# Attention and a gated MLP on one core: landing times in the plan, gated loads, second buffers, another order of block sums

## The chip, the cores and the metric

One Trainium2 chip, one core of it. The metric is the device time of the core in microseconds, from the first to the last instruction and what lies around it. Lower is better.

## The reference

Attention of 8 batches of 8 heads, 576 rows, head size 64, with keys and values averaged over groups of 8 rows (so 72 keys); its output, as 4608 rows of 512, goes through a gated MLP with 1536 hidden columns.

```python
k_p = k.reshape(B, H, Sp, pool, D).mean(axis=3)
v_p = v.reshape(B, H, Sp, pool, D).mean(axis=3)
scores = scale * np.matmul(q, k_p.transpose(0, 1, 3, 2))
attn = softmax(scores)                       # with 1e-9 added to the sum
x = np.matmul(attn, v_p)                     # (4608, 512) after a transpose
g = x @ w_gate
out = (g / (1 + np.exp(-g)) * (x @ w_val)) @ w_out
```

All arrays are float32. The kernel keeps that precision by splitting operands into a high and a low 16-bit part and adding three products.

## The kernel before

**Tiling.** The 4608 rows are nine tiles of 512 rows, the 1536 hidden columns twelve chunks of 128. A step is one chunk of one tile: gate and value products of x with that chunk's weights, tanh, and the product of both, `h`.

**Three stages.** In the first (to about 184 us) the weights are loaded and split, and tile 0 is computed whole, with an order of instructions written out by hand (`ORDER`). In the second (184 to 752 us) tiles 1 to 8 run twelve steps each, `h` is stored to DRAM (`hd`, L1138), and the attention of batches 2 to 7 runs beside the steps, in pieces of up to 128 rows. In the third, the out stage (from 752 us), the stored `h` of two tiles at a time (a pair, four pairs) is multiplied by `w_out`.

**Two ways to do a step.** A plain step (`plain_step`, lines 1026 to 1028) has 24 matmuls of 512 columns. A fast step (`fast_step`, `product`, L1116) is a seven-product scheme: seven products of six matmuls of 256 columns, 42 in all, with three ACT copies (L1172, L1174, L1181) and two DVE sums (L1177, L1182) of partial sums. It needs sums of the chunk's weights, which `fast_weights` makes once per chunk for the first `FAST` = 9 chunks (DVE L1043, POOL L1049 and L1062, ACT L1055), and sums of x, `xc`, which `fast_x` makes once per tile after x has landed (DVE L1083, L1087 on DVE or POOL, ACT L1088, L1091). A tile takes a fast step when a chunk is converted and `xc` is due soon, else a plain one. Chunks 9 to 11 are always plain.

**Attention.** `prep(b)` prepares a batch: eight loads of 0.5 MB into three `mid` buffers (`sums`, `batch_load`, L582), their sums over groups of 8 (POOL L391 to L393, DVE L386) and largest values (DVE L445) into `home["ks"]` and `home["vs"]`, a scale, and the splits of keys and values (`split_k` L457, L459, `split_v` L477 to L486) into one of two boxes, which are shared by batches b and b - 2. A piece is asked for (`ask`: queries, L600) and answered (`answer`: scores L650 and L651, softmax, a turning DMA L1290, values L776 and L777, a second turning DMA into x, L1424). The second stage has 30 such pieces, and one of batch 1.

**What sets the order.** The second and third stages are planned while the program is built: `Order` runs generators ("lines") that each yield an operation with an engine, a cost in ns and a time from which it can start; `Order.run` takes the operation that can start first, with a rank of kinds (`KINDS`) where several can, and writes it to its engine's queue. Every engine then works in that order. Buffers are pools (`get`, `put`), results are flags (`done`, `flag`). Landing times of DMAs are added by hand, for instance `t + 2500` after the store of `h`, `t + 5500` after a batch load.

**The out stage.** `sums_of_w_out` makes seven sums of w_out's blocks, each cut into a high part (ACT L1473) and a low one (POOL L1474). Per pair, `load_block` loads four blocks of h over the weights that are no longer needed, `operands` forms block differences (DVE L1569) and cuts seven operands into high (ACT L1555) and low parts (L1559: thirds 0 and 2 on DVE, 1 on POOL), two operand sets in turn, and `last_products` multiplies them (PE L1642, L1656, L1657) with PSUM copies (L1593, L1614) and adds (L1620, L1626) between.

## Time and profile before

| | |
|---|---|
| runs of the kernel, us | 983.07, 986.18, 988.71 (median 986.18) |
| the profiled execution, us | 989.56 |
| its span, first to last instruction, us | 987.7 |
| PE / DVE / ACT / POOL busy, us | 902.9 / 754.0 / 552.4 / 500.0 |
| mean granted TensorE clock | 0.973 of full |
| DMA | 159.84 MB, mean 162 GB/s |

One execution is profiled, and its times start at its first instruction. Busy time counts an instruction from its start to its end; a matmul's end is modelled, so neighbouring matmuls overlap. Idle time of an engine is put down to what released it, found from semaphores. PE is TensorE, DVE VectorE, POOL GpSimd, SP the queue that issues the DMAs.

### The profile page before, as it was taken

What the parts mean: (1) busy time and instruction counts of PE and PEld (TensorE: products, weight loads), DVE (VectorE), ACT (ScalarE), POOL (GpSimd) and SP (SyncE); (2) the same over time, 40 slices, a digit from 0 to 9 for tenths busy, and PEclk for the clock granted to TensorE, in tenths of its full rate; (3) what the DMA queues carried; (4) which work ended last, traced back from release to release, by engine and by line L of the source; (5) the groups of instructions that cost most, each with busy time, mean ns of one, the idle gap of its engine ahead of it and who ended that gap; (6) DMA issues with size and microseconds to landing.
All of it is one profiled execution on the core that took longest, in us unless ns stands there. A gap on an engine that the chain in (4) does not pass through costs nothing. (4 is left out here: it accounts for less than half of the span.)

```text
span 987.7 us, 17119 instructions
## 1 busy us (share of the span) xinstructions
PE 902.9 (91%) x6368; PEld 590.6 (60%) x6368; DVE 754.0 (76%) x1157; ACT 552.4 (56%) x1033; POOL 500.0 (51%) x519
## 2 busy tenths in 40 slices
PE   6779998598998898998798999999999999999998
PEld 5557554344446646767556768778686555555554
DVE  5789865778987997987877876755468977788684
ACT  3778873264645746674756667754456444444442
POOL 4546448067667568666586544644355322232220
PEclk9989999799999999999898999999999999999999
DMA  9865543479659439569568384451437260805401
GB/s 350 249 174 202 208 150 73 130 228 234 130 160 222 130 108 258 155 136 242 165 161 239 112 165 122 122 139 66 128 121 284 90 252 22 292 27 183 158 22 64
DMA packets 176660, 159.84 MB, mean 162 GB/s; under 512 B 115392, under 2 KB 147136, under 8 KB 172992
## 3 DMA queue, kind: packets, MB, share of 16 engines
q1 hardware_dynamic: 176576, 158.74, 54.8%
q8 instruction: 50, 0.82, 0.4%
q14 instruction: 34, 0.28, 0.1%
HBM read 95.94 MB, written 37.75 MB: 135 GB/s over the span
## 5 line engine op out<-in xcount | busy, mean ns | idle before, releaser
L1656 PE MATMUL ps<-low,wsh 128*128 128x512 bf16 x336 | 127.0, 378 | 0.0
L1026 PE MATMUL ps<-x,wgv_h 128*128 128x512 f16 x312 | 121.3, 389 | 1.9 <-DMA x<-box 1.4
L1027 PE MATMUL ps<-x,wgv_h 128*128 128x512 f16 x312 | 120.9, 387 | 0.2 <-DVE x L791 0.2
L1028 PE MATMUL ps<-x,wgv_l 128*128 128x512 f16 x312 | 120.7, 387 | 0.0
L834 ACT ACTIVATE hf<-ps,un 128x512 f32<-128x512 f32 x96 | 65.8, 685 | 84.7 <-PE ps L1028 42.1
L1116 PEld LDWEIGHTS <-mixed 128*128 128x128 f16 x1026 | 99.7, 99 | 19.4 <-issue 5.7
L1116 PEld LDWEIGHTS <-wgv_h 128*128 128x128 f16 x912 | 88.6, 99 | 29.1 <-issue 15.7
L633 POOL TENSOR_TENSOR box<-qt,box 64x512 f16<-64x512 f32 (+1 forms) x60 | 64.1, 1069 | 79.8 <-ACT box L631 62.0
L837 DVE SCALAR_TENSOR_TENSOR hf<-hf,ps 128x512 f32<-128x512 f32 x96 | 65.4, 682 | 42.3 <-ACT hf L834 42.0
L1116 PE MATMUL ps<-xc,mixed 128*128 128x256 f16 x684 | 91.4, 275 | 3.7 <-ACT ps L1174 3.6
L1116 PE MATMUL ps<-xc,wgv_h 128*128 128x256 f16 x456 | 81.3, 276 | 11.0 <-DVE ps L1182 9.9
L842 DVE SCALAR_TENSOR_TENSOR hf<-ps,un,hf 128x512 f32<-128x512 f32 x96 | 71.3, 743 | 23.8 <-PE ps L1116 15.7
L1116 PE MATMUL ps<-x,wgv_h 128*128 128x256 f16 x456 | 80.9, 275 | 1.8 <-ACT rs L1172 1.6
L1419 POOL TENSOR_TENSOR box<-sc,box 128x512 f16<-128x512 f32 (+1 forms) x30 | 37.3, 1243 | 56.9 <-ACT box L1418 48.2
L1116 PE MATMUL ps<-xc,wgv_l 128*128 128x256 f16 x228 | 63.0, 276 | 0.0
L1116 PE MATMUL ps<-x,wgv_l 128*128 128x256 f16 x228 | 62.7, 275 | 0.0
L1656 PEld LDWEIGHTS <-wsh 128*128 128x128 bf16 x336 | 32.5, 97 | 44.1 <-issue 7.4
L1559 POOL TENSOR_TENSOR low<-wgv_h,more 128x1024 bf16<-128x1024 f32 x10 | 25.8, 2579 | 63.6 <-ACT more L1555 63.6
L629 ACT ACTIVATE qt<-qt,inv 128x512 f32<-128x512 f32 (+1 forms) x60 | 40.7, 678 | 27.8 <-DMA qt<-q_twice 27.7
L1028 PEld LDWEIGHTS <-wgv_l 128*128 128x128 f16 x312 | 31.1, 100 | 39.2 <-issue 3.7
L1026 PEld LDWEIGHTS <-wgv_h 128*128 128x128 f16 x312 | 31.4, 101 | 33.0 <-issue 2.2
L1559 POOL TENSOR_TENSOR low<-wgv_h,hs 128x1024 bf16<-128x1024 f32 x10 | 24.7, 2468 | 52.1 <-ACT hs L1555 52.1
(211 smaller groups left out, 2492.2 us busy)
## 6 DMA issues: line engine op xcount, KB each, us to landing
hd<-hf SPq DMA_DIRECT2D x96, 256.0 KB, 2.5
ws<-w_all SPq DMA_DIRECT2D x12, 1536.0 KB, 7.5
qt<-q_twice SPq DMA_DIRECT2D x48, 256.0 KB, 3.5
wgv_h<-hd SPq DMA_DIRECT2D x8, 1536.0 KB, 8.7
wgv_l<-hd SPq DMA_DIRECT2D x8, 1536.0 KB, 7.9
out_t<-ob SPq DMA_DIRECT2D x36, 256.0 KB, 2.1
in<-k_rows SPq DMA_DIRECT2D x12, 576.0 KB, 5.3
in<-q_rows SPq DMA_DIRECT2D x12, 576.0 KB, 6.5
```

What stands on the lines that cost most here:

```text
L629: nc.scalar.activation(qt, qt, AF.Copy, scale=inv[:, b, 0:1])
L633: nc.gpsimd.tensor_sub(o[rows], qt[rows], o[rows])
L834: nc.scalar.activation(hf, gate, AF.Tanh, scale=un[:, c, 0:1])
L837: nc.vector.scalar_tensor_tensor(out=hf, in0=hf, scalar=1.0, in1=gate, op0=ALU.add, op1=ALU.mult)
L842: nc.vector.scalar_tensor_tensor(out=out, in0=val, scalar=un[:, c, 2:3], in1=hf, op0=ALU.mult, op1=ALU.mult)
L1026: nc.tensor.matmul(o, wh, x["h"][:, j], start=(j == 0), stop=False)
L1027: nc.tensor.matmul(o, wh, x["l"][:, j], start=False, stop=False)
L1028: nc.tensor.matmul(o, wl, x["h"][:, j], start=False, stop=(j == NJ - 1))
L1116: nc.tensor.matmul(o, a, b, start=begin and j + n == 0, stop=j == HJ - 1 and n == 2, skip_group_check=True,)
L1419: tp = yield op("POOL", 1205, lambda: nc.gpsimd.tensor_sub(xt[:, DM:], o, xt[:, :DM]), tp)
L1559: lambda: on.tensor_sub(low[:, 2 * n : 2 * n + 2], src[:, 2 * n : 2 * n + 2], rows[n].bitcast(F32)),
L1656: nc.tensor.matmul(o, top[:, c], where[1][:, c], start=False, stop=False, skip_group_check=True)
```

## The change

- **Landing times.** An operation may carry a second time: `dma` lets a load or store end for its queue after 400 ns and for who needs it after a landing time (batch loads 6500, queries 4200, blocks 9000, `h` 3000). `turn`, for turning DMAs, also lets SP be held until the last landing so far, less a margin.
- **Loads let go one by one.** A batch load takes a token (`"load": [0, 0, 0]`); each turning DMA gives one back when SP is through with it, and so does `idle` when nothing else can go on.
- **Second buffers.** `ks` and `vs` of odd batches get their own room (tag `wo2`), so `prep(b)` waits for the split of b - 2 instead of b - 1. `un`, `mt`, `r` and `ri` get more buffers. The two `rs2` sums of the out stage go to query buffers, the second buffer of `f` into the same room.
- **FAST 9 to 12.** The low parts of w_out are kept in two tiles, 9 and 3 chunks; the first is reused for the weight sums of chunks 9 to 11.
- **Sums of w_out.** The cuts are lines of their own, three of seven low parts go to DVE, the order of loads and sums changes.
- **Block sums of pairs.** The differences are formed in another order and other blocks, as a line of their own beside the cuts; low parts: thirds 0 and 1 on POOL, 2 on DVE. A new kind `seed` ranks the copies and adds that start a PSUM bank before `cut` and `out`.

```diff
-FAST = 9
+FAST = 12
-KINDS = "step", "xsum", "answer", "prep", "ask", "sums", "wsum", "load", "cut", "out"
+KINDS = "step", "xsum", "answer", "prep", "ask", "sums", "wsum", "load", "seed", "cut", "out"
...
+    def dma(self, land, f, *after, ns=400):
+        return *self.op("SP", ns, f, *after), lambda at, end: (end, at + land)
+
+    def turn(self, ns, early, land, f, *after):
+
+        def times(at, end):
+            end = max(end, self.landed - early)
+            return end, end + land
+
+        return *self.op("SP", ns, f, *after), times
...
+            if first is None and self.idle():
+                continue
...
-            self.free[engine] = at + ns
-            self.go(e, at + ns + self.LAG[engine])
+            end = done = at + ns
+            if times:
+                end, done = times[0](at, end)
+                self.landed = max(self.landed, done)
+            self.free[engine] = end
+            self.go(e, done + self.LAG[engine])
...
-            "sc": [0, 1], "pt": [0, 1], "set": [],
+            "sc": [0, 1], "pt": [0, 1], "set": [], "load": [0, 0, 0],
...
     def sums(b, i, split):
 
         n, t0 = yield get("mid")
-        t = yield op("SP", 450, lambda: batch_load(b, i, n), t0)
+        _, t1 = yield get("load")
+        t = yield dma(6500, lambda: batch_load(b, i, n), t0, t1)
         ns = {0: 2700, 1: 2386, 2: 1484}[max(0, i // 2 - 1)]
-        t = yield op("DVE" if i >= 4 else "POOL", ns, lambda: batch_sum(b, i), t + 5500, split)
+        t = yield op("DVE" if i >= 4 else "POOL", ns, lambda: batch_sum(b, i), t, split)
...
-            split = yield flag(("split", b - 1))
+            split = yield flag("room" if b == SPLIT + 1 else ("split", b - 2))
...
-        tp = 2500 + (
-            yield op("SP", 1650, lambda: turn(m, half, pt, OLD // P if old else 2 * H), tp, t0)
-        )
+        tp = yield turn_op(1450, 500, 2600, lambda: turn(m, half, pt, OLD // P if old else 2 * H), tp, t0)
+        put("load", 0, order.free["SP"])
...
+        def cut(k, g, o, t):
+            hi, lo = (a[g] for a in wpart[k])
+            t = yield op("ACT", 610, lambda: nc.scalar.copy(hi, o), t)
+            eng, ns, on = ("DVE", 800, nc.vector) if k in (1, 7, 3) else ("POOL", 1320, nc.gpsimd)
+            t = yield op(eng, ns, lambda: on.tensor_sub(lo, o, hi.bitcast(F32)), t)
+            order.done(("w cut", k, g), t)
...
-        t = yield op("SP", 450, lambda: nc.sync.dma_start(out=block[h, n], in_=src), t)
-        order.done(("block", p, h, n), t + 8000)
+        t = yield dma(9000, lambda: nc.sync.dma_start(out=block[h, n], in_=src), t)
+        order.done(("block", p, h, n), t)
...
-                eng, ns, on = (("DVE", 1230, nc.vector), ("POOL", 2550, nc.gpsimd))[n == 1]
+                eng, ns, on = (("POOL", 2500, nc.gpsimd), ("DVE", 2000, nc.vector))[n == 2]
...
+        def sums():
+            t = max((yield ready(0, 0)), (yield ready(0, 1)))
+            t = yield from less(b12, b12, b11, t)
+            order.done(("T", p, 1), t)
+            t = max(t, (yield ready(1, 1)), (yield flag(("cut", p, 5))))
+            t = yield from less(b12, b22, b12, t)
+            order.done(("T", p, 2), t)
+            t = yield from less(b11, b12, b11, t, (yield flag(("cut", p, 1))))
+            order.done(("T", p, 3), t)
+            t = yield from less(b21, b21, b12, t, (yield flag(("cut", p, 2))))
+            order.done(("T", p, 4), t)
+            t = max(t, (yield flag(("cut", p, 6))))
+            order.done(("free", p, 0, 1), t)
+
+        order.start(("cut", p), sums())
+        for k, src, when, free in (
+            (1, b11, ("block", p, 0, 0), None), (5, b12, ("T", p, 1), None), (2, b21, ("block", p, 1, 0), None),
+            (6, b12, ("T", p, 2), None), (3, b22, ("block", p, 1, 1), (1, 1)), (7, b11, ("T", p, 3), (0, 0)),
+            (4, b21, ("T", p, 4), (1, 0)),
+        ):
+            t = yield from cut(k, src, (yield flag(when)))
+            order.done(("cut", p, k), t)
+            if free:
+                order.done(("free", p, *free), t)
...
-                    order.start(prio, f)
+                    order.start(("seed", p), f)
```

## Rows read from the trace of the kernel before

**Rows 1.** The page, part 1 (busy time of each engine, share of the span, instructions) and, of part 2, the granted TensorE clock in 40 slices.
```profile
PE 902.9 (91%) x6368; PEld 590.6 (60%) x6368; DVE 754.0 (76%) x1157; ACT 552.4 (56%) x1033; POOL 500.0 (51%) x519
...
PEclk9989999799999999999898999999999999999999
```

**Rows 2.** Busy time by stretch (the windows view): stretch and its length, then busy us (instructions) of PE, PEld, DVE, ACT and POOL, granted clock, DMA share, GB/s. Five tiles of the second stage, then the last three together, then one pair of the out stage.
```profile
184.00:270.50 86.50, 81.83 (x500) 40.24 (x499) 70.53 (x127) 46.17 (x92) 53.40 (x63) 0.94 0.69 174
270.50:345.50 75.00, 66.03 (x519) 41.69 (x518) 63.39 (x114) 44.61 (x103) 48.52 (x58) 0.98 0.65 169
345.50:418.00 72.50, 68.04 (x563) 47.18 (x562) 64.47 (x105) 42.34 (x86) 51.91 (x58) 0.98 0.67 174
418.00:487.00 69.00, 61.44 (x577) 47.35 (x575) 56.32 (x105) 45.20 (x105) 42.41 (x53) 0.98 0.72 188
487.00:570.60 83.60, 74.03 (x628) 54.70 (x629) 65.31 (x129) 52.97 (x118) 56.35 (x66) 0.92 0.63 163
570.60:752.00 181.40, 177.29 (x1585) 137.72 (x1584) 116.95 (x217) 106.14 (x230) 84.85 (x92) 1.00 0.49 137
...
842.10:900.30 58.20, 56.89 (x252) 31.21 (x252) 45.37 (x34) 26.05 (x31) 16.91 (x7) 1.00 0.39 145
```

**Rows 3.** Groups of instructions by line: line, engine, operation, tiles, shapes, count | busy us, mean ns of one | idle us of the engine before them, and what ended it.
```profile
L1116 PE MATMUL ps<-xc,wgv_h 128*128 128x256 f16 x456 | 81.3, 276 | 11.0 <-DVE ps L1182 9.9 <-DVE hf L842 0.8
...
L650 PE MATMUL ps<-box 128*128 128x72 f16 (+1 forms) x240 | 25.1, 204 | 7.7 <-DVE sc L661 5.8 <-POOL box L633 1.2 <-DVE sc L781 0.4
...
L1177 DVE TENSOR_TENSOR ps<-ps,rs 128x256 f32<-128x256 f32 x57 | 24.3, 427 | 18.7 <-PE ps L1116 15.4 <-ACT qt L629 3.0 <-ACT box L1418 0.2
...
L776 PE MATMUL ps<-box,pt 128*128 128x64 f16 (+1 forms) x240 | 19.0, 197 | 11.7 <-DMA pt<-half 10.2 <-DMA qt<-q_twice 1.5
```

**Rows 4.** The chain of work that ended last, around the end of tile 7: start us, length us, what (merged where alike).
```profile
669.93 17.79 PE ps L1116 x162
...
690.33 0.22 PE ps L1026
...
690.98 0.22 PE ps L1026
```

**Rows 5.** Busy time by stretch of the fast products alone (L1116, PE): stretch and its length, busy us (matmuls), clock, DMA share, GB/s. Tiles 2 and 4.
```profile
270.50:345.50 75.00, 25.55 (x210) 0.98 0.65 169
...
418.00:487.00 69.00, 45.76 (x378) 0.98 0.72 188
```

**Rows 6.** Instructions of one line, L1062 (the last pieces of a conversion, on POOL): count: shortest/median/longest ns, start of the first and the last in us.
```profile
L1062 POOL TENSOR_TENSOR wgv_l<-fw,wgv_h x9: 662/672/1651, 215.6 to 466.2; 128x256 f16<-128x256 f32 x9
```

**Rows 7.** The same view of the two lines that issue turning DMAs, L1290 and L1424 (time that SP takes to issue one).
```profile
L1290 SPq DMA_TRANSPOSE pt<-half x31: 1240/1639/6030, 208.7 to 662.2; - x31
...
L1424 SPq DMA_TRANSPOSE x<-box x30: 1192/1233/2905, 235.6 to 670.9; - x30
```

**Rows 8.** The timeline of SP: start us, length us, queue, line, operation, what, count.
```profile
287.70 0.61 SPq L582 DMA_DIRECT2D in<-v_main  x1
...
509.93 0.49 SPq L582 DMA_DIRECT2D in<-v_main  x1
510.47 0.43 SPq L582 DMA_DIRECT2D in<-k_rows  x1
510.94 0.43 SPq L582 DMA_DIRECT2D in<-v_main  x1
511.51 2.41 SPq L1424 DMA_TRANSPOSE x<-box  x1
...
516.43 4.75 SPq L1290 DMA_TRANSPOSE pt<-half  x1
```

**Rows 9.** The timeline of DVE, PE and POOL: start us, length us, engine, line, operation, what, shapes, count, and in brackets the idle time before and what ended it.
```profile
286.04 0.99 DVE L486 SCALAR_TENSOR_TENSOR box<-box,inv 8x256 f16<-8x256 f32 x1
...
290.69 0.80 DVE L486 SCALAR_TENSOR_TENSOR box<-box,inv 8x256 f16<-8x256 f32 x1
...
517.72 2.29 DVE L386 TENSOR_REDUCE box<-in 128x72 f32<-128x576 f32 x2 [1.72 <-DMA in<-k_rows]
...
491.52 0.61 PE L1026 MATMUL ps<-x,wgv_h 128*128 128x512 f16 x1 [1.36 <-DMA x<-box]
...
508.00 2.38 POOL L1091 TENSOR_TENSOR xc<-fx,xc 128x512 f16<-128x512 f32 x2
...
784.15 2.38 POOL L1559 TENSOR_TENSOR low<-wgv_l,more 128x1024 bf16<-128x1024 f32 x1 [4.73 <-ACT more L1555]
...
785.03 3.72 DVE L1559 TENSOR_TENSOR low<-wgv_l,more 128x1024 bf16<-128x1024 f32 x2
```

**Rows 10.** Instructions of one line, L486 (the last part of a batch's split of v), columns as in rows 6.
```profile
L486 DVE SCALAR_TENSOR_TENSOR box<-box,inv x12: 483/895/1315, 205.5 to 599.0; 8x256 f16<-8x256 f32 x12
```

**Rows 11.** The same view of four kinds of instruction: the low parts of w_out's sums (L1474); who waited for the add of L1620, and how long (us in total, times); the low parts of operands (L1559) on DVE and on POOL.
```profile
L1474 POOL TENSOR_TENSOR half<-wf,wsh x6: 1262/1271/1272, 709.7 to 748.1; 128x512 bf16<-128x512 f32 x6
...
  PE ps L1642: 4.9, 4
...
L1559 DVE TENSOR_TENSOR low<-wgv_h,hs x20: 1212/1901/3395, 750.0 to 945.4; 128x1024 bf16<-128x1024 f32 x20
...
L1559 POOL TENSOR_TENSOR low<-wgv_h,hs x10: 2387/2439/2790, 751.0 to 944.5; 128x1024 bf16<-128x1024 f32 x10
```

**Rows 12.** The page, part 6: DMA issues of the first operand blocks, count, KB each, median us from issue to landing.
```profile
wgv_h<-hd SPq DMA_DIRECT2D x8, 1536.0 KB, 8.7
```

More of the change, by code (lines that the diff above doesn't have):

```diff
@@ L1030, in attention_then_swiglu, with idle @@
     x_home, xc_home = {1: (xp, "x0")}, {}
+    def idle():
+        waiting = any(e["need"] == ("get", "load") for e in order.lines)
+        if waiting:
+            put("load", 0, order.now)
+        return waiting
+    order.idle = idle
     converting, reserved = set(), {}
@@ L1487, in sums_of_w_out @@
-            t6 = yield less(a11, a22, a11, max(t3, t5c))
-            t6c = yield from cut(6, a11, t6)
-            t3 = yield less(a12, a12, a11, max(t6c, t2))
-            t = yield from cut(3, a12, t3)
+                land[m, k] = yield dma(3800, lambda: nc.sync.dma_start(out=o, in_=src), t)
+            for k, o, at_ in ((4, a22, (1, 1)), (1, a11, (0, 0)), (2, a12, (0, 1))):
+                order.start(("wsum", k), cut(k, g, o, land[at_]))
+            t = max(land[1, 0], (yield flag(("w cut", 4, g))))
@@ L1669, in last_products @@
             if k == 5:
-                where_f, trs = yield get("f")
-                rs = where_f[0].tile([P, 2, TILE], F32, name="rs2", tag=where_f[1], bufs=1)
+                trs, ways = 0, []
+                for j in range(2):
+                    way, t0 = yield get("qt")
+                    trs = max(trs, t0)
+                    ways.append(way)
+                rs = [buffer(qp, [P, TILE], F32, "rs2", "qt", at=way) for way in ways]
             o = {}
@@ L1703, in last_products @@
             t = max(t, (yield flag(("right", p, j))))
-        put("f", where_f, t)
+        for way in ways:
+            put("qt", way, t)
     def first_end(step_out, acc):
```

210 lines of the change are left out of this document (99 added, 111 removed).

## The prediction

> **What bounds the kernel now.** I read the page first: PE is busy 91% of the span, DVE 76%, and TensorE's clock dips in several slices of the middle [rows 1]. Busy time alone doesn't say what a change is worth, so I next cut the eight tiles of the second stage into windows that end where each tile's twelfth step ends [rows 2]. Two regimes show. In tiles 1 to 5 (184 to 570.6, 386.6 us) the idle time of PE is 4.7 + 9.0 + 4.5 + 7.6 + 9.6 = 35.2 us, DVE is busy 320 us (83%), and granted clocks of 0.94, 0.98, 0.98, 0.98 and 0.92 withhold 5.2 + 1.5 + 1.5 + 1.4 + 6.7 = 16 us of full clock. In tiles 6 to 8 (570.6 to 752, 181.4 us) PE idles 4.1 us, DVE is at 64% and the clock is full. The difference is attention and batch preparation, which run beside the steps and thin out after 600. So PE is the bound in the late tiles and in the out stage, and in the early tiles PE waits, with DVE close behind. What PE waits for there [rows 3]: score and value products wait for a turned block (10.2), for queries (1.5) or for DVE (5.8 at L650), fast products for DVE's evictions (9.9). In the out stage PE is busy 56.9 of 58.2 us per pair [rows 2], so little can be won there.
>
> **Part 1, three more converted chunks (FAST 12).** A plain step is 24 matmuls of (690.98 - 690.33) / 3 = 0.217 us, 5.2 us; a fast one 42 of 17.79 / 162 = 0.110, 4.61 us [rows 4]. Each replaced step saves PE 0.59 us. How many? Before, tile 2 had 210 / 42 = 5 fast steps, tiles 4 to 8 nine each, 378 / 42 [rows 5]; tile 3 had seven, the rest of 57 in all (x57, [rows 3]). Conversions are of the lowest rank: POOL's last piece of the first chunk starts at 215.6, of the ninth at 466.2 [rows 6], 31 us apart. Three more at that pace end near 560, so tile 5 gains little and tiles 6 to 8 all of it. I take 9 more fast steps (tiles 6 to 8): 9 x 0.59 = -5 us; from 6 (-3.5) to all 18 of tiles 3 to 8 (-10.6). Each new fast step adds two DVE sums of 0.43 [rows 3]: 8 us on DVE, beside PE in tiles that have DVE at 64%; if that cover were gone they would cost the 8. The conversions themselves add three chunks' work on DVE and POOL in tiles 4 to 6.
>
> **Part 2, loads and landing times.** A turning DMA is not issued until loads ahead of it are nearly down: pt<-half holds SP 1.64 us in the median and 6.03 at most [rows 7]. At 509.9 to 511 three loads go out together; the next turn takes 2.41, the one at 516.43 takes 4.75 [rows 8], and DVE stands 1.72 us in front of a load that hasn't landed [rows 9]. SP is in order, so hd stores, query fetches and further turns wait behind it; POOL's and ACT's work on queries, and then PE, wait for those. After the change each load needs a token, three at first and one more per turn issued, and goes out just behind a turn. 30 + 31 turns stand against 40 loads of batches 3 to 7, so tokens don't starve the loads as long as attention moves. The planner is also told that a turn ends only when what was issued before has landed, so it places less behind it that is wanted early. No instruction is added.
>
> **Part 3, second buffers for batch sums.** Before, a batch's sums wait until the one before is split: the loads of the next batch start at 287.70, beside the last splits at 286 to 291 [rows 8, 9], and the twelve last-part splits spread from 205.5 to 599.0 [rows 10]. Afterwards the sums of b wait for the split of b - 2 only. Scoring of b then waits less for b's preparation; the splits still wait for the box of b - 2. Work doesn't change, only when it may start. The other buffer edits (un, ri, r, mt, the parts of the low weights, rs2 in query buffers) issue the same instructions; no row shows a wait on them, and I put them at 0, between -1 and +1.
>
> **The size of parts 2 and 3.** The named waits of rows 3 that hang on turns, queries and late preparation are 10.2 + 1.5 + 5.8 + 1.2 = 18.7 us; I count two thirds gone, -13, and of the 16 us of withheld clock, which follow such pauses (487 to 570.6 has most idle time and the lowest clock, [rows 2]), 7. Together -20. The bounds: if tiles 1 to 5 became like 6 to 8 (2.3% idle, full clock), 26 + 16 = -42; if DVE at 83% is the real limit, 0, or +5 with the conversions' DVE work.
>
> **Part 4, out stage.** The set-up sums of w_out were one serial chain whose last low part starts at 748.1 [rows 11], just as tile 8 ends at 752. Three of seven low parts go to DVE and the cuts run side by side, so it ends earlier: 0, because tile 8 ends then anyway; it matters once tile 8 ends sooner. In each pair PE waits once, 4.9 us over 4 pairs, for the DVE add of L1620 that stands behind block differences [rows 11]; its new rank puts it first. That wins up to 4.9. Against it, two of three low parts of a block go to POOL, at 2.4 us where DVE takes 1.2 [rows 11]. Next: the trace has the two in each other's way. POOL works from 784.15 to 786.53, and DVE's two low parts from 785.03 take 3.72 [rows 9] where twice the shortest is 2.42; the median is 1.90 [rows 11]. If they never overlap, a pair needs 14 x 2.4 + (7 + 12) x 1.21 = 56.6 us against 56.9 of PE: no room at all. Bounds: -5 and +10. I take -3, since a pair's products leave two operand sets of 8 us each ahead. Blocks of the next pair are freed one cut sooner (0,0), and their landing (8.7 us, [rows 12]) lies under the products of 7 and 4; 0.
> The Trainium skill, page "SBUF — State Buffer", section "Who interferes with whom", says that a DVE instruction with two SBUF inputs and a GpSimd one that reads SBUF exclude each other for a whole instruction. The stretched DVE row agrees; by that rule alone the out stage would win nothing.
>
> **The sum.** -5 - 20 - 3 = -28 on the profiled execution's 989.56 gives 961.6. That execution was 3.4 above the median of the runs, 986.18; from the median it is 958.
>
> **The rivals.**
> A. DVE is the limit of tiles 1 to 5. For it: 83% busy, with in-order queues; against: DVE idled in just the places where loads were late. Then -5 - 3 and 0 to +5: about 980.
> B. Slower: no plain step is left to cover the sums of x. From x landed (PE's wait ends at 491.52) to POOL's last piece of xc (508.00 + 2.38) are 18.9 us [rows 9], and plain steps, which need no xc, now fill the start of a tile, as after 690 in tile 8 [rows 4]. If x comes no earlier, tiles 6 to 8 lose the cover of three plain steps, 15.6 us each, 47 at most; half of it is +23, the clock lost behind pauses +5, less 5 and 3: about 1004. It decides where x of a tile lands less than 19 us before the last step of the tile before. Against: the second buffers bring x forward, and x can run two tiles ahead.
> C. The out stage becomes bound by DVE and POOL excluding each other: one POOL part of 2.4 us late per pair, +10 in place of -3: about 970.
> D. The change doesn't do what it says: tokens pile up while nobody loads, so loads still go in threes, and the chunks are converted too late to count: about 984.
> E. Everything that the late tiles show is won: -42, -8, -3: about 935.
>
> **How the numbers follow.** Chances: forecast 0.50 (its own range 945 to 972), A 0.16, B 0.10, C 0.09, D 0.08, E 0.07. A measurement of this kernel tells about 0.5% from no change, 981.3 to 991.1. Faster: forecast, C, E and half of A, 0.75. Same: D's most and the rest of A, 0.12. Slower: B and what the bounds of A and C leave, 0.13. The range leaves out B and the far end of E: 940 to 984.
>
> **What would show it.** Right: turns on SP near 1.6 us with one load ahead, tiles 3 to 5 at 65 to 68 us, clock near 0.98 in tile 5, 12 fast steps in tiles 6 to 8, pairs of 57 us without the L1620 wait. Wrong: PE waiting for xc at the start of a tile (B), DVE over 88% with PE waits unchanged (A), pairs over 58.2 us with DVE low parts above 2 us (C), batch loads still in threes (D).

## The result, and the profile after

The changed kernel takes 993.24 us (median of 8 runs, 990.34 to 995.28) against 986.44 for the kernel before (8 runs): ratio 1.0067, 95% interval 1.0047 to 1.0087. Forecast were 958 and a range of 940 to 984. The profiled execution took 991.46 us (span 989.7); before, 989.56 (span 987.7).

In the changed kernel the lines have moved: plain steps are L1042 to L1044, fast products L1146, a step's last DVE instruction L852 (before L842), turns L1321 and L1453, low parts of operands L1596, block differences L1606, the sum that seeds the third product L1662, block loads L1578, loads of w_out L1517, low parts of w_out L1505. Where an experiment adds or takes lines, its numbers differ by up to three.

The page, parts 1 and 2, as in [rows 1]:

```profile
PE 902.8 (91%) x6296; PEld 583.2 (59%) x6296; DVE 749.2 (76%) x1133; ACT 550.9 (56%) x1027; POOL 607.5 (61%) x559
...
PEclk9789999789999999999899999999989899999999
```

The windows view, as in [rows 2] (stretch, length, busy us and instructions of PE, PEld, DVE, ACT, POOL, clock, DMA share, GB/s): tiles 1 to 5, then 6 and 7 together, tile 8, and one pair of the out stage.

```profile
184.00:269.10 85.10, 80.98 (x495) 40.55 (x494) 65.61 (x122) 43.09 (x86) 51.92 (x61) 0.94 0.70 189
269.10:338.50 69.40, 65.09 (x468) 37.11 (x467) 56.70 (x105) 40.78 (x87) 37.67 (x44) 1.00 0.66 182
338.50:415.20 76.70, 71.78 (x553) 44.74 (x552) 69.13 (x120) 44.35 (x92) 52.58 (x61) 0.98 0.69 180
415.20:479.50 64.30, 60.05 (x534) 41.43 (x532) 56.96 (x105) 45.06 (x102) 52.10 (x63) 1.00 0.84 221
479.50:558.70 79.20, 71.76 (x600) 49.01 (x601) 65.66 (x119) 54.06 (x117) 59.81 (x68) 0.96 0.58 143
558.70:683.00 124.30, 120.74 (x1172) 99.31 (x1171) 82.27 (x156) 75.86 (x170) 76.52 (x93) 1.00 0.47 117
683.00:750.30 67.30, 59.38 (x496) 50.23 (x494) 49.51 (x73) 35.70 (x71) 26.09 (x16) 0.95 0.40 138
846.21:903.32 57.11, 56.78 (x254) 31.32 (x253) 42.87 (x28) 25.62 (x31) 42.65 (x15) 1.00 0.40 147
```

Read length minus PE busy, then the clock. In tiles 1 to 5 PE now idles 4.1 + 4.3 + 4.9 + 4.3 + 7.4 = 25.0 us where [rows 2] gave 35.2, and the clocks withhold 5.1 + 0 + 1.5 + 0 + 3.2 = 9.8 us where they withheld 16. The early tiles did improve. By the end of tile 7 the kernel is 13.3 us ahead (683.0; before, the twelfth step of tile 7 ended at 696.3). Then it is lost: tile 8 takes 67.3 us with 7.9 idle and a clock of 0.95, where it took 55.7, so 11.6 of the 13.3 are gone at its end. From there to the first L1662 36.9 us pass (before, to L1620, 31.9): 5.1 more. The last three pairs take 59.0, 57.1 and 57.1, together 1.4 less than three of 58.2. The sum, -13.3 + 11.6 + 5.1 - 1.4, is the 2.0 us between the spans. The medians differ by more, 6.8, because the two profiled executions lie on opposite sides of theirs: 991.46 under 993.24, 989.56 over 986.44.

The cut at tile 8's end hides a part of the first pair's loss. The windows view of tile 8 and of the stretch behind it, before, then that stretch after:

```profile
696.30:752.00 55.70, 54.09 (x434) 42.38 (x433) 33.53 (x56) 30.61 (x61) 26.64 (x21) 1.00 0.49 164
752.00:783.80 31.80, 31.44 (x140) 16.98 (x140) 30.20 (x19) 16.45 (x19) 13.04 (x5) 1.00 0.29 119
```
```profile
750.30:787.30 37.00, 27.57 (x123) 14.62 (x120) 29.71 (x15) 15.64 (x18) 24.22 (x9) 0.97 0.29 110
```

After the change 23 matmuls of the first pair already run inside tile 8's window, before it was 5. So PE idles 9.4 us in front of the first pair's seeding sum, where it idled 0.4, although the stretch is only 5.1 us longer. From the end of tile 7 to that sum, a stretch called the seam below, the changed kernel takes 104.2 us and the kernel before 87.5.

**Where tile 8 stands.** The timeline of SP, then of DVE, then of PE (in brackets the idle time before, and what ended it), and one piece of the chain of waits:

```profile
711.40 0.32 SPq L1578 DMA_DIRECT2D wgv_h<-hd  x1
711.81 0.96 SPq L1578 DMA_DIRECT2D wgv_l<-hd  x1
712.87 0.43 SPq L1168 DMA_DIRECT2D hd<-hf  x1
713.61 2.10 SPq L1517 DMA_DIRECT2D wf<-wd  x4
```
```profile
716.75 0.43 DVE L1207 TENSOR_TENSOR ps<-ps,rs 128x256 f32<-128x256 f32 x1 [0.56 <-PE ps L1146]
724.80 0.86 DVE L1505 TENSOR_TENSOR wsl<-wf,wsh 128x512 bf16<-128x512 f32 x1 [7.61 <-ACT wsh L1503]
725.58 0.68 DVE L847 SCALAR_TENSOR_TENSOR hf<-hf,ps 128x512 f32<-128x512 f32 x1
726.18 0.42 DVE L1212 TENSOR_TENSOR ps<-ps,rs 128x256 f32<-128x256 f32 x1
```
```profile
726.65 0.59 PE L1146 MATMUL ps<-xc,wgv_h 128*128 128x256 f16 x2 [6.00 <-DVE ps L1212]
```
```profile
714.09 10.04 DMA wf<-wd
```

Read it backwards. PE's 6.00 us are put down to the DVE sum L1212. That sum had nothing to wait for itself; it is queued behind L1505, a low part of w_out, for which DVE stood 7.61 us. L1505 waits for ACT's high part, and that for a load of w_out which took 10.04 us, because two operand blocks of 1.5 MB each went out 2 us ahead of it. Before the change the last loads of w_out went out at 731.48 and the blocks behind them, at 738.32 (timeline of SP, before):

```profile
731.48 1.91 SPq L1468 DMA_DIRECT2D wf<-wd  x4
...
738.32 0.33 SPq L1541 DMA_DIRECT2D wgv_h<-hd  x1
```

Both kernels let the first two blocks go when tile 8 is through with chunks 0 to 5, over whose weights they are loaded (`load_block`). Before, tile 8 began with the three plain steps of chunks 11, 10 and 9, and the blocks went out as its ninth step ended (739.2). After, all twelve chunks are converted, tile 8 has no plain step, and the blocks went out between the ends of its fifth (708.3) and sixth (712.3). So 13.3 of the 27 us by which they go earlier come from tile 7's earlier end, and the rest from the three more chunks of Part 1.

**Where the first pair stands.** The timeline of DVE; the last line is the sum for which PE waits 6.99 us:

```profile
758.82 5.21 DVE L1606 TENSOR_TENSOR wgv_l<-wgv_l 128x1024 f32<-128x1024 f32 x3 [5.23 <-DMA wgv_l<-hd]
763.96 3.40 DVE L1596 TENSOR_TENSOR low<-wgv_h,hs 128x1024 bf16<-128x1024 f32 x1
767.28 6.75 DVE L1606 TENSOR_TENSOR wgv_h<-wgv_l,wgv_h 128x1024 f32<-128x1024 f32 x2
...
778.40 5.64 DVE L1606 TENSOR_TENSOR wgv_h<-wgv_h,wgv_l 128x1024 f32<-128x1024 f32 x3
783.97 3.36 DVE L1596 TENSOR_TENSOR low<-wgv_l,hs 128x1024 bf16<-128x1024 f32 x1
787.25 0.68 DVE L1662 TENSOR_TENSOR ps<-ps,rs 128x512 f32<-128x512 f32 x1
```

From 758.82 to 787.33 DVE never rests, and differences of 1.21 us each take up to 3.44.

### The profile page after: what moved, and what is told of

Same layout as the page of the kernel before. It is cut to its first block, busy times and chain, and to the rows that moved or that the text cites. A ratio compares the mean times of both kernels' runs of the same rounds, so it can differ in the third digit from the quotient of the medians.

```text
span 989.7 us, 17021 instructions
## 1 busy us (share of the span) xinstructions
PE 902.8 (91%) x6296; PEld 583.2 (59%) x6296; DVE 749.2 (76%) x1133; ACT 550.9 (56%) x1027; POOL 607.5 (61%) x559
## 4 chain that ended last, share of the span: by engine, by line
PE 65%; DVE 11%; DMA 9%; POOL 7%; issue 4%; ACT 3%; SPq 0%; POOLq 0%; DVEq 0%; ACTq 0%
PE ps L1146 17%; PE ps L1682 7%; PE ps L1697 6%; PE ps L1696 6%; PE ps L1042 6%; PE ps L1043 6%; PE ps L1044 6%; DMA pt<-half 5%; PE acc L861 2%; POOL box L643 1%; PE gv L836 1%; PE gv L838 1%; PE gv L837 1%; DMA wgv_l<-hd 1%; DVE low L1596 1%
## 5 line engine op out<-in xcount | busy, mean ns | idle before, releaser
L1042 PE MATMUL ps<-x,wgv_h 128*128 128x512 f16 x344 | 133.5, 388 | 2.5 <-DMA x<-box 1.9
L1043 PE MATMUL ps<-x,wgv_h 128*128 128x512 f16 x344 | 133.1, 387 | 0.2 <-DVE x L801 0.2
L1044 PE MATMUL ps<-x,wgv_l 128*128 128x512 f16 x344 | 133.0, 387 | 0.0
L1146 PEld LDWEIGHTS <-mixed 128*128 128x128 f16 x954 | 92.6, 99 | 16.6 <-issue 4.2
L1146 PEld LDWEIGHTS <-wgv_h 128*128 128x128 f16 x848 | 81.3, 98 | 31.9 <-issue 20.3
L852 DVE SCALAR_TENSOR_TENSOR hf<-ps,un,hf 128x512 f32<-128x512 f32 x96 | 71.3, 745 | 27.5 <-PE ps L1146 14.9
L1146 PE MATMUL ps<-xc,wgv_h 128*128 128x256 f16 x424 | 74.8, 274 | 15.5 <-DVE ps L1212 15.0
L1146 PE MATMUL ps<-xc,mixed 128*128 128x256 f16 x636 | 84.5, 274 | 1.3 <-ACT ps L1204 1.3
L1146 PE MATMUL ps<-x,wgv_h 128*128 128x256 f16 x424 | 74.4, 273 | 1.0 <-ACT rs L1202 0.9
L1596 POOL TENSOR_TENSOR low<-wgv_h,hs 128x1024 bf16<-128x1024 f32 x16 | 45.6, 2873 | 33.2 <-ACT hs L1592 33.2
L1596 POOL TENSOR_TENSOR low<-wgv_h,more 128x1024 bf16<-128x1024 f32 x16 | 47.6, 2994 | 29.4 <-ACT more L1592 29.4
L1044 PEld LDWEIGHTS <-wgv_l 128*128 128x128 f16 x344 | 34.2, 99 | 42.9 <-issue 3.7
L1146 PE MATMUL ps<-xc,wgv_l 128*128 128x256 f16 x212 | 58.1, 274 | 0.0
L1146 PE MATMUL ps<-x,wgv_l 128*128 128x256 f16 x212 | 57.8, 273 | 0.0
L1043 PEld LDWEIGHTS <-wgv_h 128*128 128x128 f16 x344 | 34.2, 99 | 37.4 <-issue 5.3
L1042 PEld LDWEIGHTS <-wgv_h 128*128 128x128 f16 x344 | 34.5, 100 | 34.9 <-issue 2.2
```

The costliest lines, as they stand in the source:

```text
L852: nc.vector.scalar_tensor_tensor(out=out, in0=val, scalar=un[:, c, 2:3], in1=hf, op0=ALU.mult, op1=ALU.mult)
L1042: nc.tensor.matmul(o, wh, x["h"][:, j], start=(j == 0), stop=False)
L1043: nc.tensor.matmul(o, wh, x["l"][:, j], start=False, stop=False)
L1044: nc.tensor.matmul(o, wl, x["h"][:, j], start=False, stop=(j == NJ - 1))
L1146: nc.tensor.matmul(o, a, b, start=begin and j + n == 0, stop=j == HJ - 1 and n == 2, skip_group_check=True,)
L1596: lambda: on.tensor_sub(low[:, 2 * n : 2 * n + 2], src[:, 2 * n : 2 * n + 2], rows[n].bitcast(F32)),
```

## The experiments

Times are medians, ratios (with 95% intervals) are to the kernel before, run beside it on the same chip. Where an interval holds 1, no difference is shown.

**1. Operand blocks behind the loads of w_out.**

```diff
+ t = max(t, (yield flag("w loads")))     # first pair's load_block
...
+ if g == 2: order.done("w loads", order.free["SP"])   # after the last loads of w_out
```


> The changed kernel (993.2 us), with one edit: the first pair's four operand blocks are not loaded before the last loads of w_out's sums are issued. Theory 1 (3 MB of operand blocks issued at 711.4 and 711.8 hold the loads of 713.6 back; DVE stands 7.6 us in front of them, PE 6.0 us): that wait of PE and the half clock behind it are gone, tile 8 takes about 57 us in place of 67.3, the whole 983 to 986. Rival (the low parts that went to DVE are what DVE stands at, whenever the loads land): the wait stays near 6 us, the whole 991 to 994.


987.57, ratio 1.0026 (1.0007 to 1.0045). Tile 8, in the windows view:

```profile
686.90:746.40 59.50, 57.26 (x495) 49.21 (x495) 50.09 (x73) 35.70 (x71) 25.94 (x16) 1.00 0.44 155
```

7.8 us shorter with the same matmuls, 2.2 idle instead of 7.9, full clock. DVE, ACT and POOL have the same order of instructions in both kernels, SP alone another, so the order of the loads is the cause of tile 8's stall. What tile 8 still takes above the 55.7 of before is no stall: 22 matmuls of the first pair run inside it. The median lies just above the expected range, and the first pair still waits 7.00.

Up to tile 7's end this kernel has the order of the changed one, yet its tile 7 ends at 686.9, not at 683.0. Nine kernels here share that order (the changed one and experiments 1, 2, 3, 8, 11, 13, 14 and 17), and their nine profiled executions end tile 7 between 682.9 and 687.5, in the median at 684.5. That is how much one execution tells.

**2. All low parts of w_out on POOL** (none on DVE).

> The changed kernel, with all low parts of w_out's sums on POOL again (three of seven were on DVE). Theory 1 (the loads are late): DVE now stands at the sums of the same late loads instead, PE still waits 4 us or more, the whole 990 to 994. Rival (DVE's share of low parts): the wait of 6 us is gone, tile 8 takes about 57 us, the whole 983 to 986.


991.57, ratio 1.0052 (1.0025 to 1.0079), tile 8 at 68.6 us. Taking the waiting instruction off DVE helps nothing while the load is late: the waits of tile 8 only become three of 3.60, 1.85 and 1.43.

**3. Low thirds of operands as before** (0 and 2 on DVE, 1 on POOL).

> The changed kernel, with the low thirds of operands on the engines of before (0 and 2 on DVE, 1 on POOL); the new order of block sums and the new ranks stay. Theory 2 (DVE and POOL parts with two SBUF inputs exclude each other; in the first pair the differences stretch from 1.21 to 3.4 us): the 7.0 us wait at 781 shrinks to under 2, differences are back near 1.21, steady pairs take 57 to 58.2 in place of 57.1; the whole 987 to 991. Rival (the second row of blocks lands late, at 758.8, and the new order needs it sooner): the first pair still waits 5 us or more.


985.65, ratio 1.0000 (0.9978 to 1.0023). Both expectations failed in part. The differences are back at 1.21 us in the median, and the time is better than the range, but the first pair's wait shrinks only to 5.07, the sign of the rival. By the trace two thirds on POOL cost 2.7 us in tile 8, 3.1 in front of the first seeding sum (33.8 for 36.9) and 2.5, 0.8 and 0.7 in the three pairs behind it (56.5, 56.3 and 56.4 for 59.0, 57.1 and 57.1); 1.5 of it is given back at the end.

**4. Nine converted chunks** (`FAST = 9`).

> The changed kernel, with FAST 9 in place of 12. Theory 3 (three more chunks delay no one, conversions are late because batch sums now come first): about as many fast steps as now in tiles 2 to 6 and three plain ones more in tiles 7 and 8, so 49 to 53 fast steps and +1 to +4, the whole 994 to 997, less what tile 8 gains where plain steps cover the late loads. Rival (the three chunks themselves starve the first nine): 57 or more fast steps, tiles 2 to 6 shorter by 4 or more, the whole 986 to 989.


982.79, ratio 0.9981 (0.9966 to 0.9996), so 10 us less than the changed kernel and better than both expectations. That looked like the price of the three chunks. The timeline of SP shows another reason: with plain steps left in tile 8, chunks 0 to 5 are through later, and the blocks go out behind the loads of w_out.

```profile
707.51 1.91 SPq L1517 DMA_DIRECT2D wf<-wd  x4
719.10 0.32 SPq L1578 DMA_DIRECT2D wgv_h<-hd  x1
```

That accounts for a part. Experiment 1 mends the loads too and keeps twelve chunks, and nine are 4.8 us faster than that; what this rest is, no run shows.

**5. No gate** (a hundred tokens for three).

> The changed kernel, but with a hundred tokens for the large loads of batches instead of three, so that they go out as soon as their place is free, as before the change; the planner keeps the measured landing times and the second buffers. Open question: which part of the change shortened tiles 1 to 7 by 13.3 us (tile 7 ends at 683.0, before at 696.3). If the letting go one by one did it: loads go out in groups of two and three again, the turns' time on SP above the usual 1.64 and 1.23 us grows from 16 us back towards the 31 us of before, tile 7 ends at 690 or later, and the time is 1.010 to 1.017 of before. If the second buffers did it: turns get longer but PE doesn't wait for them, tile 7 ends within 3 us of 683, ratio 1.004 to 1.010.


986.69, ratio 1.0015 (0.9996 to 1.0034); tile 7 ends at 679.8. The turns do get longer (their SP time above the usual is 24.6 us, 16.2 with the gate), but the kernel is no slower. In this order the last four loads of w_out go out behind one block, not two, and tile 8 takes 64.4 us for 67.3.

**6. One buffer for batch sums.**

```diff
- split = yield flag("room" if b == SPLIT + 1 else ("split", b - 2))
+ split = yield flag(("split", b - 1))
```


> The changed kernel, but the sums of a batch wait again until the batch before is split, so the second buffers are not used ahead of time; tokens and landing times stay. If the second buffers gave the 13 us of tiles 1 to 7: tile 7 ends at 692 or later, ratio 1.010 to 1.020. If the letting go one by one gave it: tile 7 ends near 683. Second question: why the ninth chunk of the weights is converted at 573 and not at 466. If earlier batch sums take DVE's and POOL's free time from the conversions, the ninth conversion returns to 460 to 500 and there are more than 60 fast steps instead of 53; if the planner's landing times or the wait for the room are the cause, the conversions stay within 20 us of the changed kernel's.


1010.05, ratio 1.0235 (1.0194 to 1.0276). Tile 7 ends at 700.0, 17 us later, and PE's waits for turned blocks are back (groups of instructions; first the changed kernel, then this one):

```profile
L786 PE MATMUL ps<-box,pt 128*128 128x64 f16 (+1 forms) x240 | 18.4, 194 | 2.5 <-DMA pt<-half 2.5
```
```profile
L786 PE MATMUL ps<-box,pt 128*128 128x64 f16 (+1 forms) x240 | 18.9, 196 | 11.2 <-DMA pt<-half 11.1
```

The ninth conversion returns to 483.6 (573.5 in the changed kernel) and there are 63 fast steps, not 53. So the earlier batch sums are what delays the conversions. The gate is kept here, but with one buffer it doesn't hold: batch loads go out in threes 7 times, in the changed kernel never, so this run loses what the gate does as well.

**7 and 8. The mended kernel** (experiments 1 and 3 together) with nine chunks, and with twelve.

> The changed kernel with three of its parts mended: operand blocks of the first pair wait until the loads of the output weights are issued, nine converted chunks instead of twelve, and the low thirds of a block on DVE, POOL, DVE as before the change. If the three losses are separate (8 us of tile 8 by the loads, 3 to 6 by the low thirds, 3 to 7 by the three chunks) they add up to 13 to 18 us: 975 to 980, ratio 0.988 to 0.993, faster than both. If they are one loss seen three times (whatever ends tile 8 sooner is lost in front of the first pair, where the set-up sums of the output weights or the second block row decide), it is no better than the best of the three alone, 982 to 985.

> As the combined kernel, but with twelve converted chunks as in the change. With the loads out of the way of tile 8 the three late chunks can be judged alone. If each fast step saves 0.59 us, the 5 more fast steps of tiles 7 and 8 make it 2 to 3 us faster than the combined kernel. If what they save is eaten by their conversions on DVE and POOL in tiles 6 and 7 and by two DVE sums of each step, it is 0 to 5 us slower.


980.58 with nine (0.9943; 0.9924 to 0.9961), 979.54 with twelve (0.9924; 0.9896 to 0.9953). The two losses are separate and add: alone they gave back 5.7 and 7.6, together 13.7. So do they in the trace, where the seam takes 104.2 us in the changed kernel, 96.9 and 98.4 in experiments 1 and 3, and 91.2 here with twelve chunks. Tiles 7 and 8 take 116.6 us with twelve and 119.4 with nine, but PE is busy 114.6 and 114.2 of them: the difference is idle time, and this pair of kernels doesn't measure what a fast step saves. With both mended, nine chunks or twelve make 1.0 us.

**9. The mended kernel without the gate.**

> The twelve-chunk mended kernel (979.54), with a hundred tokens for the large loads instead of three. In the changed kernel taking the gate away ended tile 7 at 679.8 instead of 683.0. If the gate itself costs (loads held back while the queues are free), the same 3 to 5 us appear here: 973 to 977. If that was only another order that happened to come out better, the time lies at 977 to 985 here.


979.21, ratio 0.9923 (0.9890 to 0.9956): the same. The 6.5 us of experiment 5 were another order, not the gate's price. The gate does what it was made for: in experiment 8 batch loads stand alone on SP in 36 of 38 places, here in 24 of 31 (before the change, in 12 of 23), and PE's value products wait 3.4 us for turned blocks there, here 8.1. In time the gate is worth nothing either way.

**10. Conversions ahead of batch sums.**

```diff
- order.start(("wsum", 0), fast_weights())
+ order.start(("sums", 0), fast_weights())
```


> The twelve-chunk mended kernel, with the conversions of weight chunks ranked ahead of the batch sums instead of behind them. If late conversions are what cost Part 1 its gain: the ninth conversion returns from 578 to under 470, there are 63 or more fast steps instead of 53, and PE saves 0.59 us for each of the 10, so 970 to 976. If the free time of DVE and POOL in tiles 1 to 5 is what is short, the sums are late instead, score steps wait for prepared batches, tile 7 ends later than 687.5, and the time is 980 to 995.


1001.45, ratio 1.0156 (1.0119 to 1.0193). All fast products, then tiles 3 to 5 of this kernel and of the mended one (windows view):

```profile
184.00:770.00 586.00, 369.48 (x3150) 0.95 0.60 158
...
339.30:585.60 246.30, 204.33 (x2009) 168.13 (x2010) 210.13 (x401) 165.87 (x372) 174.33 (x202) 0.91 0.67 171
```
```profile
338.00:562.80 224.80, 205.48 (x1687) 135.94 (x1686) 190.56 (x341) 143.48 (x310) 163.28 (x190) 0.97 0.69 175
```

3150 / 42 = 75 fast steps, 22 more, and PE has no more to do, but these three tiles take 21.5 us longer: 42 us idle instead of 19, and the clock falls to 0.91. Among the waits are 9.36 us for a turned block at 423.55 and 7.63 for POOL at 508.38. DVE is busy 85% in both. The conversions do come early, the ninth at 365.5, and the time still lies beyond both expectations. The early tiles have no room for the conversions.

**11. The last difference later, in all pairs.**

```diff
- t = yield from less(b21, b21, b12, t, (yield flag(("cut", p, 2))))
+ t = yield from less(b21, b21, b12, t, (yield flag(("cut", p, 2))), (yield flag(("begun", p, 3, 1))))
```


> The twelve-chunk mended kernel, with the last difference of a block pair (three DVE instructions, for the product that comes last) held until the sums that seed the third product are done. In the first pair PE waits 5.19 us at 774.35 for the DVE sum at L1665, which stands behind these differences and low parts on DVE. If that order is the cause, the wait shrinks to 1 to 2 us and the time is 975 to 977; if DVE's own load in front of the first pair is (it idles nowhere between 756 and 782), the wait moves to another product, 978 to 981.


983.44, ratio 0.9977 (0.9961 to 0.9992). The first pair's wait is gone (tile 8's end to L1665: 28.3 us for 34.0), but each later pair gets two waits, 1.67 and 1.82, and takes 60.3 to 60.8 us. The time misses both expectations.

**12. A control:** the changed kernel with 760 ns instead of 757 for one DVE cost in the plan.

> A control: the changed kernel, where the planner takes 760 ns instead of 757 for the DVE instruction that ends a step. Nothing else is edited and no work is changed, but the order that the planner writes out is another one in all later stages. If the orders are worth the same whatever such small costs are, the time is 990 to 996, ratio 1.004 to 1.010. If one order differs from the next by chance, it may lie anywhere from 980 to 1005, and differences of a few us between the kernels here say nothing unless a wait in the trace goes with them.


992.28, ratio 1.0064 (1.0035 to 1.0093): the same time by another way. Tile 7 ends at 687.5 and tile 8 takes 62.2. Here too the last four loads of w_out go out behind one block. A single tile says little; the total held.

**13. The old order of block sums in the mended kernel.**

> The twelve-chunk mended kernel (979.54), with the block sums and cuts of the out stage in the order of before: one chain, second differences behind the cuts. Its pairs take 56.7 us and its first pair 34.0 from the end of tile 8 to the first sum that seeds the third product; before the change they took 58.2 and 31.9. If the new order is worth the 1.5 us of each of three pairs and costs the 2 us of the first: three pairs near 58.2, the first near 32, time 981 to 984. If the low thirds and loads set both and the order nothing: 978 to 981, pairs at 56.7.


973.68, ratio 0.9873 (0.9848 to 0.9898): the fastest here, faster than both kernels. Both expectations failed, since the pairs stay at 56.7 and the first takes 26.9 us. The timeline of DVE, first of the mended kernel, then of this one:

```profile
768.71 4.53 DVE L1609 TENSOR_TENSOR wgv_h<-wgv_h,wgv_l 128x1024 f32<-128x1024 f32 x2
773.16 1.21 DVE L1599 TENSOR_TENSOR low<-wgv_l,hs 128x1024 bf16<-128x1024 f32 x1
774.29 1.21 DVE L1609 TENSOR_TENSOR wgv_h<-wgv_h,wgv_l 128x1024 f32<-128x1024 f32 x1
775.43 3.36 DVE L1599 TENSOR_TENSOR low<-wgv_l,hs 128x1024 bf16<-128x1024 f32 x1
778.71 0.69 DVE L1665 TENSOR_TENSOR ps<-ps,rs 128x512 f32<-128x512 f32 x1
```
```profile
771.28 1.21 DVE L1609 TENSOR_TENSOR wgv_l<-wgv_l 128x1024 f32<-128x1024 f32 x1
772.41 0.68 DVE L1660 TENSOR_TENSOR ps<-ps,rs 128x512 f32<-128x512 f32 x1
773.01 1.21 DVE L1609 TENSOR_TENSOR wgv_l<-wgv_l 128x1024 f32<-128x1024 f32 x1
774.14 0.69 DVE L1660 TENSOR_TENSOR ps<-ps,rs 128x512 f32<-128x512 f32 x1
```

The new order puts the difference for the last product (wgv_h<-wgv_h,wgv_l) ahead of the seeding sum; in the old one only that for the last product but one is due there, and the seeds slip in between. From the end of tile 7 on, no wait of PE is longer than 0.8 us. By the trace the old order gives 3.2 us in the seam (88.0 for 91.2). The medians, of four and five runs, differ by 5.9; of the 6.9 us between the two profiled spans, 3.1 lie ahead of the seam, where both kernels have the same order, and are chance.

**14. The last difference later, in the first pair only.**

> The twelve-chunk mended kernel, with the last difference held behind the sums that seed the third product in the first pair only. In all pairs this took PE's 5 us wait from the first pair and gave each later pair 3.5 us of new waits (pairs of 60.3 us for 56.7). If the two effects are separate, the first pair keeps the gain of some 3 to 5 us less its own two new waits of 1.7 and 1.8, the later pairs stay at 56.7, and the time is 976 to 979. If the later pairs inherit the first one's lateness through the block loads: 979 to 983.


982.72, ratio 0.9970 (0.9947 to 0.9994). The second expectation held: the first pair's wait moves to the second (4.65 us at 831.55).

**15 and 16. Without the landing times.** First all of Part 2 undone, with nine chunks; then only the rule that holds a turn until earlier loads have landed, with twelve. Both without the gate. Of the edit, the line that both take out:

```diff
- end = max(end, self.landed - early)
```


> The combined kernel with nine chunks (980.58), with Part 2 undone as a whole: a hundred tokens, and the planner again takes the landing times of before the change (loads 5.5, queries 3.0, stores 2.5, turns 1.65 and 1.5 us, a turn held by nothing). The second buffers stay. If Part 2 is worth nothing: 978 to 984, tile 7 ends near 680. If the measured landing times are what made the second buffers pay: tile 7 ends at 688 or later and the time is 986 or more.

> The mended kernel with twelve chunks and without the gate (979.21), with one more edit: the planner no longer takes a turn to end only when what was issued before has landed. The other landing times stay. If that rule is worth something beside an open gate, tile 7 ends at 685 or later (680.8) and the time is 983 to 990. If not, 976 to 982.


1004.47 (1.0193; 1.0149 to 1.0236) and 988.08 (1.0023; 1.0010 to 1.0037), where the kernels that keep the landing times take 980.58 (with the gate) and 979.21. Tile 7 ends at 700.4 and 694.0, not at 680. PE's wait for turned blocks is 15.6 us over 8 waits in the first; with landing times and no gate it is 8.1, in the changed kernel 2.5. A part of the loss goes with late conversions: 41 and 45 fast steps, where the kernels that keep the landing times have 48 and 51.

**17. The seeds without their rank,** in the kernel of experiment 13.

```diff
- order.start(("seed", p), f)
+ order.start(prio, f)
...
```


> The mended kernel with the old order of block sums (973.68), where the sums that seed the third product lose their new rank ahead of the block differences and cuts. If the rank is what shortens pairs from 58.2 to 56.7 and takes the 5 us from the first pair: pairs of 58 us or more, first pair 30 to 32 instead of 26.9, time 979 to 984. If other things did it: 972 to 976.


981.71, ratio 0.9956 (0.9929 to 0.9983), so 8.0 us for the rank: by the trace 2.3 in front of the first seeding sum (29.2 for 26.9) and 5.0 in the three pairs behind it. One pair without it, then with it (windows view), and the seed without it, behind three differences (timeline of DVE):

```profile
833.60:891.80 58.20, 56.59 (x247) 31.22 (x252) 45.36 (x35) 26.05 (x31) 16.92 (x7) 1.00 0.40 145
```
```profile
828.60:885.30 56.70, 56.33 (x249) 31.31 (x253) 46.41 (x34) 25.93 (x30) 18.84 (x7) 1.00 0.40 149
```
```profile
771.99 3.48 DVE L1609 TENSOR_TENSOR wgv_l<-wgv_l 128x1024 f32<-128x1024 f32 x3
775.39 1.28 DVE L1660 TENSOR_TENSOR ps<-ps,rs 128x512 f32<-128x512 f32 x2
```

**18. A control on the kernel before** (760 ns for 757).

> A control: the kernel before, where the planner takes 760 ns instead of 757 for the DVE instruction that ends a step. No work is changed; the order is another one. If the kernel before was not a lucky order: tile 7 ends at 691 to 701 and the time is 982 to 991. If it was a lucky one, tile 7 ends at 702 or later and the time is 993 or more, and part of what the changed kernel lost is only the loss of that luck; if an unlucky one, tile 7 ends before 690 and the time is below 980.


989.36, ratio 1.0025 (0.9998 to 1.0051). Its profiled execution, the shortest of its ten at 982.88, ends tile 7 at 688.9. So an order and an execution can move that point by some 7 us. The time is within the expected range, tile 7 ends earlier than expected. From 184 us to the end of tile 7 PE idles 37.3 us here and 37.7 in the kernel before, but the clock withholds 8 us here and 17 there.

## Why the prediction was wrong, by its own steps

The steps that failed are Part 4's "0" for the sums of w_out, its "-3" for the out stage, and Part 1's count of fast steps.

**Parts 2 and 3 (-20): the size was about right, the reason half.** Idle time of PE in tiles 1 to 5 fell by 10.2 of the 13 forecast, withheld clock by 6.2 of 7. The idle time is the change's, as far as one control tells: up to the end of tile 7 the kernel before and its control idle 37.7 and 37.3, the nine executions of the changed order 28.6 to 32.4. The clock's share isn't shown: the control on the kernel before withholds 8, those nine 8 to 14, so that the 6.2 may be chance, and the forecast luckily near. The prediction gave it to loads let go one by one and to second buffers each for itself. The runs show that the gate is worth nothing in time (experiments 5 and 9), and that second buffers and landing times pay only together: without the buffers tile 7 ends at 700.0, without the landing times at 700.4, with both between 679.8 and 687.5 in the changed kernel and in thirteen of its versions (all but that with conversions first, 707.3). These fourteen executions hold four orders up to there: the changed one nine times, that of nine chunks twice, that without the gate twice, and the control. The two undone parts lie 12 us and more beyond all of them. For the gap to the kernel before itself, 13.3 us, the controls leave room (688.9 and 687.5 differ by 1.4), so its size is less sure than that of the two undone parts.

**Part 1 (-5): the price was right, the count wrong.** A fast product still takes 40.04 / 366 = 0.109 us after the change (the chain of waits), so that a step saves about 0.6:

```profile
646.73 40.04 PE ps L1146 x366
```

The count came from the conversions' pace before the change, "three more at that pace". The pace fell, because Part 3 puts batch sums, of a higher rank, into the same free time of DVE and POOL: the ninth conversion starts its last piece at 573.5, before at 466.2 [rows 6]. The windows view of the fast products after the change, tiles 1 to 5 and tiles 6 to 8:

```profile
184.00:558.70 374.70, 105.12 (x879) 0.97 0.69 182
558.70:752.00 193.30, 154.64 (x1349) 0.98 0.45 127
```

These are 20.9 and 32.1 fast steps, where the prediction's count before was 30 and 27: 53 for 57, so by its own price +2.4 instead of -5 (an estimate, 4 x 0.59). Two parts of one change drew on one reserve, and the prediction costed each as if it had it alone. Experiments 6 and 10 show both sides of that trade.

**Part 4, sums of w_out (0): the step that cost most.** "0, because tile 8 ends then anyway" looked at when the chain ends and not at what its loads meet. Tile 8 lost 11.6 us. Experiment 1 returns 7.8 of them in the trace and 5.7 in the median by the order of six DMAs alone. The prediction named the stall to come on PE's side (late x) and on DVE's (the low parts), but no load. It had the fact in hand: rival B says that with twelve chunks tile 8 has no plain steps to start with. It asked what that does to the sums of x, and not when the weights of chunks 0 to 5 come free for the blocks. So Part 1 has a share in the loss that Part 4 put at nothing; with nine chunks (experiment 4) the blocks do go out later.

**Part 4, out stage (-3).** The rank of the seeds was put at "up to 4.9" and is worth more, 8.0 in the median (experiment 17), since to the 5.0 of the three later pairs it adds 2.3 in the first. The two things set beside it were mis-sized. The new order of the differences was costed at nothing, with only its earlier block loads in view; it costs 5.9 in the median (979.54 to 973.68, experiment 13) and 3.2 in the seam by the trace, in front of the first pair's seed, where differences for later products stand; the later pairs are the same. The low thirds on POOL, rival C, cost 7.6 in the median (experiment 3), by the trace 2.7 in tile 8, 3.1 in front of the first pair's seed and 4.0 in the three pairs behind it, less 1.5 at the end. Against a forecast of -3 the stage gave -1.4 in three pairs and +5.1 in the first. The prediction took its pairs from a steady one, and the first pair, which starts with no operand sets ahead, has no such cover.

**The rivals.** A, DVE as the limit, is out for the waits, which did fall, and right about the room: in tiles 1 to 5 DVE is busy 84% after the change, and the conversions found no place (experiment 10). B, the slower one, was a wrong mechanism: PE waits for xc nowhere, and no tile starts so. C had the right cause and a fitting size, but more than half of it falls ahead of the first pair's seed. D was half true: the loads no longer go in threes, yet that changes nothing in time, and the chunks come late. Two of the rivals' sums are slightly off: B's terms give 1006, not 1004, and E's 933, not 935. The slower result has two causes that no rival named, the order of the loads and the order of the differences; both are orders in the written-out program, and both lie at the seam between stages, of which the prediction read hardly a row.

**The sum, as measured.** Tiles 1 to 7 -13.3, tile 8 +11.6, first pair +5.1, other pairs -1.4, in the profiled executions. The seam, +16.7 in all, comes back step by step: the two mends of experiment 8 take it from 104.2 to 91.2, the old order of differences to 88.0, and before the change it was 87.5. With both orders mended and the thirds put back, the rest of the change is worth 12.4 us (986.10 to 973.68).

What stays open: how much of the 13.3 us belongs to the change and how much to the order and the clock; why the gate's shorter waits bring no time; and why the medians put the order of differences at 5.9 where the seam shows 3.2.

## What to carry to other kernels

When a change starts work earlier, ask what its loads are issued ahead of: a large load 2 us in front of a small urgent one cost more than the idle time it was to fill. Cost parts that use the same engine's free time together, not one by one, and read the seam between two stages as a stage of its own. Where a planner writes the order, run a control with an immaterial cost, and believe a difference only when a wait in the trace goes with it.

## What the runs showed of the hardware

Subtractions on DVE and POOL slow each other by more than the prediction's one row. The 48 differences of L1606 (groups view) take 29.2 + 25.0 + 22.2 + 17.2 = 93.6 us; the 48 of L1569 took 27.9 + 13.9 + 13.9 = 55.7. The dearest group of after on DVE, and one on POOL:

```profile
L1606 DVE TENSOR_TENSOR wgv_h<-wgv_h,wgv_l 128x1024 f32<-128x1024 f32 x12 | 29.2, 2488 | 0.0
...
L1596 POOL TENSOR_TENSOR low<-wgv_h,more 128x1024 bf16<-128x1024 f32 x16 | 47.6, 2994 | 29.4 <-ACT more L1592 29.4
```

In this group a difference of 1212 ns becomes 2488 in the mean, over all 48 about 2000. POOL's part of the same tiles, 2579 in the mean before, becomes 2994. The Trainium skill, page "SBUF — State Buffer", section "Who interferes with whom", has such instructions exclude each other for a whole instruction. The traces agree: the longest of these DVE instructions, up to 3.44 us, are about 1.21 plus most of a POOL one. By its rule alone the prediction had the out stage win nothing; it lost 3.7 in the trace, with the first pair counted.

A load of w_out takes 4.3 us from issue to landing in the median and up to 10.3 behind the two blocks. And a late load stopped an engine that doesn't read it: DVE stood 7.61 us for a low part of w_out, and PE 6.00 for a sum that stood behind it in DVE's queue.

The turns mostly bear out the prediction's reading of SP: of the ten longest of the kernel before, seven (6.03 to 3.44 us) end 0.1 to 0.5 us before a load that was issued ahead of them lands; three end earlier.
